# Network two with six steps of sevens: stores of outputs asked for a place later, gates ahead of low parts, casts for w_out's sums at other places

## The chip, the cores and the metric

The kernel runs on one core of one Trainium2 chip. The metric is device time in microseconds, from the first to the last instruction with what lies around them, as the median of several runs. A core has five engines with a queue each: TensorE (PE; its weight loads are shown as PEld), VectorE (DVE), ScalarE (ACT), GpSimd (POOL) and SyncE (SP, which here only issues DMAs). In the trace each engine's rows stand in the order in which the program gives them; engines wait for each other by semaphores.

## The reference

```python
def reference(**kwargs):
    ...
    x = attn_out            # X = fft(fft(x, axis=1), axis=2).real, x is 4 x 3072 x 256
    x = _moe_ref(x=x, **moe_kwargs)      # a gated network, width 1024
    x = x.reshape(B * S, x.shape[-1])
    return _moe2_ref(x=x, **moe2_kwargs)

def _moe2_ref(x, w_in, w_out):
    h = x @ w_in            # 12288 x 256 by 256 x 2048
    g = h - np.tanh(h)
    return (g @ w_out).astype(np.float32)   # 12288 x 2048 by 2048 x 256
```

The change touches the last of the three stages only, `_moe2_ref`, called network two here.

## The kernel before

The kernel runs in three stages: the transform, network one, network two. Every fp32 product is made of three fp32r matmuls (`mm3`, lines L395 to L397): high part by high, high by low, low by high. So each operand is split into a high part (a cast, `hi`, on ScalarE, L1081) and a low part (a subtraction, `lo`, on VectorE or GpSimd, L1083).

Network two works on 12 items `n` of 1024 tokens, and on each in 8 steps `q` of 256 hidden units. A step computes a 2x2 block of h by Strassen's scheme with seven products instead of eight: left operands `a11 a12 s1 s2 s3 a22 s4`, right operands in `TI`, all accumulating in four PSUM banks (two banks `x`, which alternate from step to step, one bank `z`, one bank `w`). The step then applies the gate h - tanh(h): `bend` is the tanh on ScalarE (L1072), and a subtraction on VectorE follows. Six of the eight steps, q = 0, 1, 3, 4, 6, 7, are "sevens": their product with w_out is made by seven products too (weights `W7`), which needs sums and differences of the gated blocks. The two others, q = 2 and 5, are plain (weights `WO`). In the last item q = 7 is plain too.

The order of all work is written out by hand in `step`. A step finishes its blocks 21 and 12 only while the next step runs; the leftovers are called by name through `late(...)`:

- `t21`, `g21`: tanh and gate of block 21, which lies in the old bank x. `c12`, `t12`, and `g12` or `G12`: the sum, tanh and gate of block 12, which lies in bank w.
- `l22`: the low part of block 22, read from bank z by VectorE. `f22`: a copy of the same block from bank z into SBUF by ScalarE (L1216).
- `s3`, `s1` (L1226): differences and sums with block 21 on VectorE; `s1` is added into the old bank x itself. `+s2`, `+s4` and `S4`: the other sums.
- `hs1`, `ls1` and so on, `ha12`, `LA12`: the high and low parts of those operands.

By what came before it a step has one of three forms. In form "b" both previous steps are sevens (q = 0, 1, 2, 5). In form "c" the previous step is plain (q = 3, 6). In form "e" the previous one is a seven and the one before it is plain (q = 4, 7). The steps q = 0 and 5 follow an "e"; q = 1 and 2 follow a "b". In the first item that `step` does, n = 1, q = 0 is a "c", q = 1 an "e" and q = 2 a "b". So there are 42 steps of form "b" in all: four in each of the items 2 to 11, two in item 1. Of these 20 follow a "b" and 22 an "e".

Early in each step the line `A.copy(Z, X)` (L1110) seeds bank z with the first product, and z must be free of the previous step's block 22 for it. In a "b" step the products `k1` (`apart`, tiles named `k`) are written into the previous step's bank x, which is free only once `s1`'s low part, `ls1`, has read it. Near the end of a step `V.tensor_add(Z, Wb, s3)` (L1180) makes block 22, and its tanh, gate and cast follow.

`fill()` stands four times in a step and runs what was put down for the next slot of a calendar: loads of `TI` for later steps (L1247, from `stream`), the left operands of the next item, the weights `W7` (`seven`: casts on ScalarE, L429, and six subtractions on GpSimd, L430 and L516 to L519). Item 1 begins at slot 32 of network two. Outputs are stored by `send` (L1034, a DMA of 256 KB on SP's queue), called by `part` and `whole_out`.

```python
        P(X, "s3")
        ...
        s3 = copied(X)
        ...
        P(Wb, "s1", True)
        ...
        V.tensor_add(Z, Wb, s3)
        t22 = bend(Z)
```

Of the kernel before, what the change touches and what calls it, by code (L numbers as in the profile page):

```python
# [406 lines left out]
class Kernel:  # L407
# [622 lines left out]
                self.V.tensor_add(self.acc[key], self.acc[key], K)  # L1030
        return add

    def send(self, n, t, h, a):
        self.nc.sync.dma_start(out=self.out[n, t, :, h], in_=a)  # L1034

    def part(self, n, t, h, eng=None):

# [19 lines left out]
    def step(self, n, q):  # L1057

        V, A, T, G = self.V, self.A, self.T, self.G
# [3 lines left out]
        seven = q in self.sevens(n)  # L1063
        one, two = (bool(p and p["seven"]) for p in (p1, p2))
        form = "b" if one and two else "c" if not one else "e"
        group = lambda p, o: [o, p] if p["q"] in (1, 4, 7) else [p]
        def P(ps, k, start=False):
            i = RIGHT[k]
            mm3(T, ps, [W[:, 0, i], W[:, 1, i]], [S[k][:, 0], S[k][:, 1]], start)
        def bend(src):  # L1070
            t = self.room(self.act, "c", "c", 4)
            A.activation(t, src, TANH)  # L1072
            return t
        def copied(src):
            t = self.room(self.act, "s", "s", 3)
            A.copy(t, src)  # L1076
            return t
        M, st = {}, {}
        def hi(k, src):
            M[k] = self.operand(k, *self.span(n, q, k))  # L1080
            A.copy(M[k][:, 0], src)  # L1081
        def lo(k, src, eng):
            eng.tensor_sub(M[k][:, 1], src, M[k][:, 0].bitcast(F32))  # L1083
        late = lambda *names: [p1["late"][k]() for k in names]
        new = lambda name: self.room(self.kp, "xt", name, 4)
        nop = lambda: None
        k1 = k2 = None
        if one and self.last(p1["n"], p1["q"]) == p1["q"]:
            g = group(p1, p2)
            k1, k2 = (lambda: self.apart(g, "a11")), (lambda: self.apart(g, "s1"))  # L1090
        if two and self.last(p2["n"], p2["q"]) == p2["q"]:
            g = group(p2, p3)
            k1, k2 = (lambda: self.apart(g, "s2")), (lambda: self.apart(g, "s3"))
        self.odd ^= 1
        X, Z = self.bank(f"x{self.odd}", "x"), self.bank("z", "z")
# [3 lines left out]
        elif form == "c":  # L1099
            self.whole(p1, "11", (0,))  # L1100
        P(X, "a11", True)
        if one:
            late("l22")
        late("t21")
        if form != "b":
            late("c12")
        if one:
            late("f22")
        late("g21")
        A.copy(Z, X)  # L1110
        if form == "b":
            self.direct(p2, "s4")
            if (n, q) == (1, 2):
                self.direct(p2, "a22")
            self.direct(p1, "a22")
            late("s3", "s1", "+s2", "hs3", "hs1", "c12", "t12")
        elif form == "c":
            self.whole(p1, "11", (1,))
            self.whole(p1, "22", (0,))
            late("t12", "h21", "g12")  # L1120
            if q == 3 and n > 1:
                self.part(n - 1, 1, 1)
            late("l21", "h12")
        else:
            self.whole(p2, "21")
            late("t12", "s3", "s1", "+s2", "hs1")
        P(Z, "a12")
        if form == "b":
            late("ls1", "ls3", "g12")
        elif form == "c":  # L1130
            late("l12")
        else:
            late("G12", "hs3", "ls3", "ls1", "ha12", "LA12")
        P(X, "s2")
        if form == "e":
            late("S4")
        t11 = bend(Z)
        s2 = copied(X)
        if form == "b":
            late("ha12", "la12", "+s4")  # L1140
        if q == 1 and n > 1:
            self.part(n - 1, 0, 0)
        if (n, q) == (1, 1):
            self.part(0, 1, 0)
            self.part(0, 1, 1, A.copy)
# [5 lines left out]
                self.direct(p1, "a22")  # L1151
            self.whole(p2, "12", (0,))
        add = k1() if k1 else nop
        if seven and form == "e":
            g = st["11"] = new("g11")
            V.tensor_sub(g, Z, t11)
            hi("a11", g)
            lo("a11", g, G)
        else:
            V.tensor_sub(Z, Z, t11)  # L1160
            hi("a11" if seven else "11", Z)
        add()
        P(X, "s3")
        if seven and form != "e":
            st["11"] = new("g11")
            A.copy(st["11"], Z)
        s3 = copied(X)
        if not (seven and form == "e"):
            lo("a11" if seven else "11", Z, V)
        if one:  # L1170
            late("hs2", "ls2")
        self.fill()
        Wb = self.bank("w", "w")
        P(Wb, "s1", True)
# [4 lines left out]
            self.whole(p2, "12", (1,))  # L1179
        V.tensor_add(Z, Wb, s3)  # L1180
        t22 = bend(Z)
        if one:
            late("hs4", "ls4")
        if q == 1 and n > 1:
            self.part(n - 1, 0, 1)
            self.whole_out(n - 1, 0, 1)
# [54 lines left out]
    def phase2(self):  # L1241
        A, V = self.A, self.V
        z0 = 16 * NP
        self.W7, self.C, self.acc, self.older, self.oldest = {}, {}, {}, None, None
        def stream(g):
            t = self.w1.tile([128, 2, 7, 128], F32R, tag="T", name="TI", bufs=4)
            self.nc.sync.dma_start(out=t.rearrange("p s k n -> p (s k n)").bitcast(F32), in_=self.ti[g % 8])  # L1247
            self.TI[g] = t
        for g in range(8, 8 * NP):
            self.at(z0 + 4 * (g - 1), lambda g=g: stream(g))  # L1250
        self.TI = dict(enumerate(self.TI))
        for j in range(3, 8):
            self.weights2(z0 + 4 * (j - 2), j, self.kp, "xt", 4)
        xt, ring = (self.kp, "xt", 4), (self.w1, "T", 4)
        t4 = (lambda: self.p2b, lambda: self.p2a)
        for i, (q, slot, src) in enumerate(((0, 24, xt), (1, 27, xt), (3, 30, xt), (4, 33, xt), (6, 36, (self.p2a, "wf", 1)), (7, 54, (self.p2a, "wf", 1)))):
            self.seven(z0 + slot, q, *((self.p2a, f"TI{i}", 1) if i < 4 else ring), *src, t4[i % 2])
        for n in range(NP):
            for q in range(8):
                if n == 0 and q == 1:  # L1260
                    self.xctx.close()
                    self.p2b = self.ctx.enter_context(self.tc.tile_pool(name="p2b", bufs=1, side="right", reuse_waits="tile"))
                    self.homes = [[self.p2a, "WO0", 1, 1.5], [self.p2a, "WO1", 1, 2.5], [self.p2a, "WO3", 1, 4.5], [self.w1, "WR", 1, 0.], [self.p2b, "M", 2, 1.], [self.p2b, "M", 2, 1.1],
                                  [self.wvp, "wv", 4, 5.6], [self.wvp, "wv", 4, 7.6], [self.wvp, "wv", 4, 9.8]] + [[self.act, "m", 4, t] for t in (8.3, 8.6, 9.3, 9.8)]
                if q == 1 and n + 1 < NP:
                    u = self.left2(n + 1)
                    names = "a11 a12 a22 +s1 +s3 +s2 +s4 s1 s3 s2 s4".split()
                    when = (7, 8, 11, 12, 12, 15, 16, 16, 19, 20, 22) if n == 0 else (12, 12, 13, 14, 14, 15, 24, 24, 25, 26, 27)
                    self.at(z0 + 32 * n + (8 if n else 5), u["load"])
                    for k, name in zip(when, names):  # L1270
                        self.at(z0 + 32 * n + k, u[name])
                if n:
                    self.step(n, q)
                else:
                    w2 = [[self.WO[q][:, s, 256 * c:256 * c + 256] for s in range(2)] for c in range(2)]
                    self.quad(2, n, q, 8, self.S2[n], self.TI.pop(q), w2, None)
                if (n, q) == (NP - 1, 3):
                    self.at(self.now + 1, *self.plain(7))
            if n == 0:
                self.pend["seven"] = False  # L1280
                self.C.update({(0, t, h): self.O[t][h] for t in range(2) for h in range(2)})
        p, w, n, G = self.pend, self.older, NP - 1, self.G
        late = lambda *names: [p["late"][k]() for k in names]
        a11, h, s2, t = (self.acc[n, k] for k in ("a11", "h", "s2", "t"))
        self.direct(w, "a12")
        K = self.bank(f"x{1 - self.odd}", "k")
        L = self.bank("z", "l")
        def extra(ps, k):
            a, m = self.product(w, k)
            mm3(self.T, ps, a, [m[:, 0], m[:, 1]])  # L1290
        extra(K, "s2")
        late("t21", "c12")
        V.tensor_add(s2, s2, K)
        V.tensor_add(t, t, K)
        late("t12", "g21")
        G.tensor_add(s2, s2, h)
        self.whole(p, "11")
        extra(L, "s3")
        late("h21", "g12", "l21", "h12", "l12")
        V.tensor_add(t, t, L)  # L1300
        self.whole(p, "22")
        G.tensor_add(h, h, t)
        self.direct(w, "s4")
        V.tensor_add(t, t, a11)
        self.whole(p, "21")
        for k, (i, a) in enumerate((((1, 0), t), ((1, 1), h), ((0, 0), a11), ((0, 1), s2))):
            if k == 2:
                self.whole(p, "12")
            V.tensor_add(a, a, self.C.pop((n, *i)))
            self.send(n, *i, a)  # L1310

    def plain(self, q):

# [115 lines left out]
```

## Time and profile before

| | before |
|---|---|
| median of 3 runs | 1671.08 us (1670.69 to 1671.22) |
| the profiled execution's own time | 1669.62 us |
| its span, first to last instruction | 1667.8 us |
| mean granted clock of TensorE | 0.998 |
| PE busy | 1616.8 us, 97% of the span |
| DVE, ACT, POOL busy | 82%, 77%, 67% |

The profiled execution is 1.46 us under the median of the runs, and 1.82 us of its time lie outside its span. Matmuls are pipelined, and a row's duration is longer than the distance to the next one; the busy share of PE therefore hides short waits. The count of matmuls in a stretch, or the distance from start to start, shows them. In the timeline views the columns are start, duration (both us), engine, line, operation, tiles written and read; in brackets the idle time of the engine before the row and what ended it.

### The profile page before, as it was taken

To read this page: it belongs to the slowest core of one execution; us is meant where nothing else is said; L and a number is where in the kernel's file an instruction comes from. 1 tells how busy PE (TensorE), PEld (TensorE's weight loads), DVE (VectorE), ACT (ScalarE), POOL (GpSimd) and SP (SyncE) were. 2 spreads that over 40 slices of the span, in tenths; PEclk is the share of its full clock that TensorE was granted. 3 is DMA by queue.
4 is the path that set the end of the run, shared out by engine and by line. 5 is a ranking of instruction groups with operands and counts; after the bars stand their busy time and mean duration, and the time that the engine had idled before them with its cause. 6 is when DMAs were issued, how large, how long until landed. Compare 5 with 4: busy or idle time off the path is not lost.

```text
span 1667.8 us, 22306 instructions
## 1 busy us (share of the span) xinstructions
PE 1616.8 (97%) x7283; PEld 1299.4 (78%) x7283; DVE 1360.9 (82%) x2115; ACT 1279.7 (77%) x2464; POOL 1111.4 (67%) x928
## 2 busy tenths in 40 slices
PE   8999999999999999999999999999999999999998
PEld 7978888888888887877777777777777777777776
DVE  7987888888898887777788878888788887888787
ACT  5887777777777777877878787878777878787875
POOL 1166667676666666767776767676767676767653
PEclk9999999999999999999999999999999999999999
DMA  9620111101111132444242424241414141414140
GB/s 334 170 58 26 46 45 64 34 30 57 52 58 64 45 108 90 176 137 144 79 149 77 151 75 153 73 155 69 159 67 161 67 161 67 162 66 161 67 164 26
DMA packets 59348, 168.74 MB, mean 101 GB/s; under 512 B 6864, under 2 KB 15824, under 8 KB 59232
## 3 DMA queue, kind: packets, MB, share of 16 engines
q1 hardware_dynamic: 57648, 162.87, 28.8%
q0 software_dynamic: 1440, 4.46, 1.6%
q8 instruction: 57, 0.93, 0.2%
q14 instruction: 59, 0.48, 0.1%
q10 hardware_dynamic: 144, 0.00, 0.0%
HBM read 128.43 MB, written 38.86 MB: 100 GB/s over the span
## 4 chain that ended last, share of the span: by engine, by line
PE 27%; DVE 16%; ACT 9%; DMA 2%; issue 1%; DVEq 0%; POOLq 0%; SPq 0%; ACTq 0%
ACT s L1081 4%; PE k L395 3%; PE k L397 3%; DVE a L1083 3%; PE k L396 3%; ACT a L1081 3%; DMA TI<-ti 2%; DVE g L1226 2%; PE x L395 2%; PE o L395 2%; PE o L397 2%; DVE x L1212 2%; PE o L396 2%; PE x L397 2%; PE x L396 2%; DVE z L1180 1%
## 5 line engine op out<-in xcount | busy, mean ns | idle before, releaser
L1083 POOL TENSOR_TENSOR s<-g,s 128x512 fp32r<-128x512 f32 x195 | 250.5, 1296 | 7.1 <-ACT s L1081 7.0
L1227 POOL TENSOR_TENSOR g<-g,g 128x512 f32<-128x512 f32 x107 | 138.7, 1296 | 113.4 <-DVE x L1226 67.6
L696 POOL TENSOR_TENSOR s<-xk,s 128x512 fp32r<-128x512 f32 x94 | 125.2, 1332 | 87.8 <-ACT s L694 82.7
L696 POOL TENSOR_TENSOR a<-xk,a 128x512 fp32r<-128x512 f32 x70 | 92.3, 1328 | 123.7 <-ACT a L694 123.6
L396 PE MATMUL o<-m,wv 128*128 128x512 f32 x384 | 149.7, 390 | 0.0
L397 PE MATMUL o<-m,wv 128*128 128x512 f32 x384 | 149.7, 390 | 0.0
L395 PE MATMUL o<-m,wv 128*128 128x512 f32 x384 | 149.6, 390 | 0.0
L1072 ACT ACTIVATE c<-z 128x512 f32<-128x512 f32 x176 | 105.5, 600 | 33.7 <-DVE z L1180 33.1
L1081 ACT CAST s<-g 128x512 fp32r<-128x512 f32 x195 | 120.9, 620 | 6.2 <-DVE g L1226 5.8
L1076 ACT COPY s<-x 128x512 f32<-128x512 f32 x176 | 104.2, 592 | 19.7 <-PE x L397 17.9
L1083 POOL TENSOR_TENSOR a<-g,a 128x512 fp32r<-128x512 f32 x64 | 82.8, 1294 | 39.9 <-ACT a L1081 39.8
L571 ACT ACTIVATE c<-z 128x512 f32<-128x512 f32 x112 | 67.2, 600 | 54.7 <-DVE z L660 54.5
L578 DVE TENSOR_TENSOR m<-z,m 128x512 fp32r<-128x512 f32 x112 | 76.8, 686 | 32.7 <-ACT m L576 32.7
L1192 DVE TENSOR_TENSOR z<-z,c 128x512 f32<-128x512 f32 x88 | 61.6, 700 | 46.3 <-ACT c L1072 44.6
L1083 DVE TENSOR_TENSOR a<-z,a 128x512 fp32r<-128x512 f32 x108 | 74.6, 691 | 24.3 <-ACT a L1081 14.7
L430 POOL TENSOR_TENSOR xr<-xt,xr 128x512 fp32r<-128x512 f32 x46 | 60.7, 1327 | 46.4 <-ACT xr L429 46.3
L395 PE MATMUL x<-s,TI 128*128 128x512 f32 x192 | 77.9, 406 | 13.6 <-ACT s L1076 13.3
L1180 DVE TENSOR_TENSOR z<-w,s 128x512 f32<-128x512 f32 x88 | 61.6, 700 | 35.6 <-ACT s L1076 26.3
L576 ACT CAST m<-z 128x512 fp32r<-128x512 f32 x112 | 65.8, 587 | 28.3 <-DVE z L664 23.5
L1081 ACT CAST a<-z 128x512 fp32r<-128x512 f32 x108 | 63.7, 590 | 29.9 <-DVE z L1192 23.2
L395 PE MATMUL x<-a,TI 128*128 128x512 f32 x192 | 76.9, 400 | 8.5 <-DMA TI<-ti 6.9
L396 PEld LDWEIGHTS o<-m,wv 128*128 128x128 f32 x384 | 72.1, 188 | 15.7 <-DVE m L578 0.5
(1019 smaller groups left out, 5815.0 us busy)
## 6 DMA issues: line engine op xcount, KB each, us to landing
TI<-ti SPq DMA_DIRECT2D x88, 896.0 KB, 5.5
spill<-r SPq DMA_DIRECT2D x48, 256.0 KB, 2.6
xk<-spill SPq DMA_DIRECT2D x48, 256.0 KB, 5.4
out<-o SPq DMA_DIRECT2D x44, 256.0 KB, 2.4
ti<-TI SPq DMA_DIRECT2D x8, 896.0 KB, 4.8
wf<-wf SPq DMA_DIRECT2D x17, 256.0 KB, 2.8
raw<-w_in SPq DMA_DIRECT2D x32, 128.0 KB, 2.2
cv<-w_out SPq DMA_DIRECT2D x16, 256.0 KB, 3.1
```

The lines of the kernel that those rows point to most:

```text
L395: T.matmul(ps, w[0], m[0], start=start, stop=False, skip_group_check=True)
L396: T.matmul(ps, w[0], m[1], start=False, stop=False, skip_group_check=True)
L397: T.matmul(ps, w[1], m[0], start=False, stop=stop, skip_group_check=True)
L571: A.activation(t, src, ACT.Tanh if ph == 2 else ACT.Relu)
L578: V.tensor_sub(M[blk][:, 1], g, M[blk][:, 0].bitcast(F32))
L696: eng.tensor_sub(S[name][:, 1], src(), S[name][:, 0].bitcast(F32))
L1072: A.activation(t, src, TANH)
L1076: A.copy(t, src)
L1081: A.copy(M[k][:, 0], src)
L1083: eng.tensor_sub(M[k][:, 1], src, M[k][:, 0].bitcast(F32))
L1180: V.tensor_add(Z, Wb, s3)
L1227: "+s2": lambda: G.tensor_sub(g("22"), g("22"), g("11")), "+s4": lambda: G.tensor_sub(g("12"), g("12"), g("22")),
```

## The change

The change does five things, all in network two.

1. `send` no longer issues its DMA at once; it puts it down for a later `fill()`, except for the last four outputs.
2. In form "b" the order `l22`, `t21`, `f22`, `g21` becomes `t21`, `g21`, `l22`, `f22`. So VectorE does block 21's gate ahead of block 22's low part.
3. In form "e" the high and low parts of `s1` are made after the gate and the casts of block 11, no longer at the head of the step; the cast `ha12` comes after the tanh of block 11; the gate of block 11 comes ahead of `LA12` and `S4`; and `hs4`, `ls4` change places with `hs2`, `ls2`.
4. The first part of an item's output, in q = 1, is added up after the sum of `k1` and no longer ahead of block 11's gate.
5. The six sets of `W7` are made at other slots: 23, 26, 29, 40, 45, 54 in place of 24, 27, 30, 33, 36, 54, and the fourth is loaded through another buffer.

```diff
-    def send(self, n, t, h, a):
-        self.nc.sync.dma_start(out=self.out[n, t, :, h], in_=a)
+    def send(self, n, t, h, a, now=False):
+        f = lambda: self.nc.sync.dma_start(out=self.out[n, t, :, h], in_=a)
+        f() if now else self.at(self.now + 1, f)
...
         P(X, "a11", True)
-        if one:
-            late("l22")
         late("t21")
-        if form != "b":
-            late("c12")
-        if one:
-            late("f22")
-        late("g21")
+        if form == "b":
+            late("g21", "l22", "f22")
+        elif form == "e":
+            late("l22", "c12", "f22", "g21")
+        else:
+            late("c12", "g21")
         A.copy(Z, X)
...
             self.whole(p2, "21")
-            late("t12", "s3", "s1", "+s2", "hs1")
+            late("t12", "s3", "s1", "+s2", "hs3", "ls3")
         P(Z, "a12")
...
-            late("G12", "hs3", "ls3", "ls1", "ha12", "LA12")
+            late("G12")
         P(X, "s2")
+        t11 = bend(Z)
+        side = seven and form == "e"
+        def gate():
+            if side:
+                st["11"] = new("g11")
+            V.tensor_sub(st["11"] if side else Z, Z, t11)
         if form == "e":
-            late("S4")
-        t11 = bend(Z)
-        s2 = copied(X)
+            late("ha12")
+            gate()
+            s2 = copied(X)
+            late("LA12", "S4")
+        else:
+            s2 = copied(X)
         if form == "b":
             late("ha12", "la12", "+s4")
-        if q == 1 and n > 1:
-            self.part(n - 1, 0, 0)
...
+        hi("a11" if seven else "11", st["11"] if side else Z)
+        if side:
+            lo("a11", st["11"], G)
+        if form == "e":
+            late("hs1", "ls1")
         add()
+        if q == 1 and n > 1:
+            self.part(n - 1, 0, 0)
         P(X, "s3")
...
-        if one:
+        if form == "b":
             late("hs2", "ls2")
+        elif form == "e":
+            late("hs4", "ls4")
...
-        if one:
+        if form == "b":
             late("hs4", "ls4")
+        elif form == "e":
+            late("hs2", "ls2")
...
-        for i, (q, slot, src) in enumerate(((0, 24, xt), (1, 27, xt), (3, 30, xt), (4, 33, xt), (6, 36, (self.p2a, "wf", 1)), (7, 54, (self.p2a, "wf", 1)))):
+        for i, (q, slot, src) in enumerate(((0, 23, xt), (1, 26, xt), (3, 29, xt), (4, 40, wf), (6, 45, wf), (7, 54, wf))):
```

How the built program's order changes is shown at three places. The first is VectorE in a "b" step that follows an "e", from block 22's sum (L1180 before, L1190 after) to the low part of `s1`. Tile a22 is the low part `l22`, the row that writes x from x and c is `g21`. Before, and then in the change:

```order
L1180 TENSOR_TENSOR z_12229<-w_12295,s_12290 128x512
L1192 TENSOR_TENSOR z_12229<-z_12229,c_12303 128x512
L1083 TENSOR_TENSOR a22_12309<-z_12229,a22_12309 128x512
L1212 TENSOR_TENSOR x_12228<-x_12228,c_12326 128x512
L1226 TENSOR_TENSOR g11_12282<-g11_12282,x_12228 128x512
L1226 TENSOR_TENSOR x_12228<-x_12228,g22_12328 128x512
L1209 TENSOR_TENSOR w_12295<-w_12295,s_12272 128x512
L1083 TENSOR_TENSOR s1_12343<-x_12228,s1_12343 128x512
```

```order
L1190 TENSOR_TENSOR z_12229<-w_12295,s_12290 128x512
L1204 TENSOR_TENSOR z_12229<-z_12229,c_12303 128x512
L1224 TENSOR_TENSOR x_12228<-x_12228,c_12325 128x512
L1084 TENSOR_TENSOR a22_12309<-z_12229,a22_12309 128x512
L1238 TENSOR_TENSOR g11_12266<-g11_12266,x_12228 128x512
L1238 TENSOR_TENSOR x_12228<-x_12228,g22_12329 128x512
L1221 TENSOR_TENSOR w_12295<-w_12295,s_12268 128x512
L1084 TENSOR_TENSOR s1_12343<-x_12228,s1_12343 128x512
```

The low part of block 22 now stands behind the gate of block 21; nothing else moved on VectorE here. ScalarE's order in a "b" step is the same in both programs: cast of a22, tanh `t21`, copy `f22`, the seed of z (L1110), casts of s3 and s1.

The second place is ScalarE in an "e" step, from the tanh `t12` (it reads w) to the tanh of block 22. Rows that write s from x are `copied(X)`, first after the product s2, then after the product s3. Before, and then in the change:

```order
L1072 ACTIVATE c_12247<-w_12193 128x512
L1081 CAST s1_12252<-x_12124 128x512
L1081 CAST s3_12258<-g11_12185 128x512
L1081 CAST a12_12262<-w_12193 128x512
L1072 ACTIVATE c_12270<-z_12229 128x512
L1076 COPY s_12272<-x_12228 128x512
L1081 CAST a11_12284<-g11_12282 128x512
L1076 COPY s_12290<-x_12228 128x512
L1081 CAST s2_12292<-g22_12237 128x512
L1072 ACTIVATE c_12303<-z_12229 128x512
```

```order
L1073 ACTIVATE c_12247<-w_12193 128x512
L1082 CAST s3_12252<-g11_12185 128x512
L1073 ACTIVATE c_12262<-z_12229 128x512
L1082 CAST a12_12264<-w_12193 128x512
L1077 COPY s_12268<-x_12228 128x512
L1082 CAST a11_12281<-g11_12266 128x512
L1082 CAST s1_12284<-x_12124 128x512
L1077 COPY s_12290<-x_12228 128x512
L1082 CAST s4_12292<-g12_12271 128x512
L1073 ACTIVATE c_12303<-z_12229 128x512
```

The cast of s1 moved from the head to behind the cast of a11, the tanh of block 11 moved ahead of the cast of a12, and s4 and s2 changed places.

The third place is SP's queue of DMA issues around q = 1 of an item; out is a store, TI a load of weights, xk a load of the next item. Before, and then in the change:

```order
L1247 DMA TI_12366<-ti 128x1792
L1034 DMA out<-o_12468 128x512
L1247 DMA TI_12471<-ti 128x1792
L1034 DMA out<-o_12511 128x512
L1034 DMA out<-o_12406 128x512
L1247 DMA TI_12578<-ti 128x1792
L916 DMA xk_12580<-spill 128x512
```

```order
L1259 DMA TI_12366<-ti 128x1792
L1259 DMA TI_12468<-ti 128x1792
L1034 DMA out<-o_12481 128x512
L1034 DMA out<-o_12510 128x512
L1259 DMA TI_12577<-ti 128x1792
L916 DMA xk_12579<-spill 128x512
L916 DMA xk_12581<-spill 128x512
L916 DMA xk_12583<-spill 128x512
L916 DMA xk_12585<-spill 128x512
L1034 DMA out<-o_12406 128x512
```

The first store of the item went behind the load of TI that it stood ahead of, and the third went behind the next load of TI and the four loads of xk.

## Rows read from the trace of the kernel before

**Rows 1.** Busy time in two stretches; counts in brackets, then clock, DMA share, GB/s.

```profile
300.00:400.00 100.00, 100.00 (x442) 82.32 (x441) 84.58 (x128) 74.74 (x139) 67.79 (x56) 1.00 0.16 51
...
1200.00:1300.00 100.00, 96.53 (x409) 74.85 (x408) 79.70 (x123) 79.62 (x148) 73.78 (x58) 1.00 0.33 111
```

**Rows 2.** Waits of TensorE over the whole run: total us, times, longest us.

```profile
PE x L395 <- ACT s L1076: 13.9, 24, 1.5
...
PE x L395 <- DMA TI<-ti: 6.9, 10, 2.1
```

**Rows 3.** Timeline of VectorE, an "e" step and three "b" steps, item around 1230 us.

```profile
1229.65 0.68 DVE L1222 TENSOR_TENSOR g<-w,g 128x512 f32<-128x512 f32 x1
...
1232.10 0.70 DVE L1180 TENSOR_TENSOR z<-w,s 128x512 f32<-128x512 f32 x1 [1.17 <-ACT s L1076]
...
1234.82 0.69 DVE L1083 TENSOR_TENSOR a<-z,a 128x512 fp32r<-128x512 f32 x1 [0.66 <-ACT a L1081]
1235.42 0.69 DVE L1212 TENSOR_TENSOR x<-x,c 128x512 f32<-128x512 f32 x1
...
1236.82 0.69 DVE L1226 TENSOR_TENSOR x<-x,g 128x512 f32<-128x512 f32 x1
...
1238.17 0.69 DVE L1083 TENSOR_TENSOR s<-x,s 128x512 fp32r<-128x512 f32 x1
...
1242.11 0.70 DVE L1180 TENSOR_TENSOR z<-w,s 128x512 f32<-128x512 f32 x1
...
1252.72 0.70 DVE L1180 TENSOR_TENSOR z<-w,s 128x512 f32<-128x512 f32 x1
```

**Rows 4.** Timeline of TensorE and its weight loads (PEld), the same stretch.

```profile
1229.09 0.39 PE L397 MATMUL o<-12_12149,WO 128*128 128x512 f32 x1
1230.04 0.50 PE L395 MATMUL x<-s,TI 128*128 128x512 f32 x1 [0.56 <-ACT s L1076]
...
1238.92 0.50 PE L395 MATMUL k<-a,W 128*128 128x512 f32 x1 [0.42 <-DVE s L1083]
...
1248.93 0.50 PE L395 MATMUL k<-s,W 128*128 128x512 f32 x1 [0.20 <-DVE s L1083]
...
1259.55 0.19 PEld L395 LDWEIGHTS k<-a,W 128*128 128x128 f32 x1 [0.40 <-DVE s L1083]
```

**Rows 5.** Timeline of ScalarE, the first of these "b" steps.

```profile
1234.68 0.61 ACT L1072 ACTIVATE c<-x 128x512 f32<-128x512 f32 x1
1235.60 0.59 ACT L1216 COPY g<-z 128x512 f32<-128x512 f32 x1 [0.31 <-DVE a L1083]
1236.22 0.57 ACT L1110 COPY z<-x 128x512 f32<-128x512 f32 x1
...
1237.55 0.59 ACT L1081 CAST s<-x 128x512 fp32r<-128x512 f32 x1
```

**Rows 6.** Line L1216, whole run: what ended ScalarE's idle time before it (us, times).

```profile
  DVE a L1083: 12.1, 42
```

**Rows 7.** Timeline of ScalarE, the "e" step ahead of them.

```profile
1227.42 0.59 ACT L1081 CAST s<-x 128x512 fp32r<-128x512 f32 x1 [0.84 <-DVE x L1226]
...
1229.38 0.60 ACT L1076 COPY s<-x 128x512 f32<-128x512 f32 x1
...
1231.49 0.58 ACT L1076 COPY s<-x 128x512 f32<-128x512 f32 x1
```

**Rows 8.** Timeline of SP, q = 1 of the same item.

```profile
1250.18 0.34 SPq L1034 DMA_DIRECT2D out<-o  x1
1250.61 0.38 SPq L1247 DMA_DIRECT2D TI<-ti  x1
```

**Rows 9.** Timelines of item 1, around its q = 1 and 2: VectorE, GpSimd, weight loads.

```profile
748.44 0.70 DVE L1180 TENSOR_TENSOR z<-w,s 128x512 f32<-128x512 f32 x1 [1.17 <-ACT s L1076]
...
753.17 1.31 POOL L430 TENSOR_TENSOR W<-t,W 128x512 fp32r<-128x512 f32 x1
...
756.91 0.19 PEld L395 LDWEIGHTS k<-a,W 128*128 128x128 f32 x1
```

More of the change, by code (lines that the diff above doesn't have):

```diff
@@ L1153, in step @@
         add = k1() if k1 else nop
[L1154 to L1161, printed above, removed]
+        if form != "e":
+            gate()
+        hi("a11" if seven else "11", st["11"] if side else Z)
[3 more added lines that the diff above has]
+            late("hs1", "ls1")
         add()
+        if q == 1 and n > 1:
+            self.part(n - 1, 0, 0)
         P(X, "s3")
-        if seven and form != "e":
+        if seven and not side:
             st["11"] = new("g11")
@@ L1167, in step @@
         s3 = copied(X)
-        if not (seven and form == "e"):
+        if not side:
             lo("a11" if seven else "11", Z, V)
-        if one:
+        if form == "b":
             late("hs2", "ls2")
+        elif form == "e":
+            late("hs4", "ls4")
         self.fill()
@@ L1253, in phase2 @@
             self.weights2(z0 + 4 * (j - 2), j, self.kp, "xt", 4)
-        xt, ring = (self.kp, "xt", 4), (self.w1, "T", 4)
+        xt, wf, ring = (self.kp, "xt", 4), (self.p2a, "wf", 1), (self.w1, "T", 4)
         t4 = (lambda: self.p2b, lambda: self.p2a)
-        for i, (q, slot, src) in enumerate(((0, 24, xt), (1, 27, xt), (3, 30, xt), (4, 33, xt), (6, 36, (self.p2a, "wf", 1)), (7, 54, (self.p2a, "wf", 1)))):
+        for i, (q, slot, src) in enumerate(((0, 23, xt), (1, 26, xt), (3, 29, xt), (4, 40, wf), (6, 45, wf), (7, 54, wf))):
             self.seven(z0 + slot, q, *((self.p2a, f"TI{i}", 1) if i < 4 else ring), *src, t4[i % 2])
@@ L1309, in phase2 @@
             V.tensor_add(a, a, self.C.pop((n, *i)))
-            self.send(n, *i, a)
+            self.send(n, *i, a, True)
     def plain(self, q):
```

## The prediction

> **What bounds the kernel now.** I read the stretches first. In network one TensorE starts 442 matmuls in 100 us, one each 0.226 us, and never waits; in network two it starts 409 in the same time [rows 1]. So in network two some 33 x 0.226 = 7.5 us of each 100 are lost, though TensorE looks 96.5% busy. Network two takes about 920 us, so about 65 us is all that a reordering can win, and any reordering can add to it.
>
> Then I looked for where the loss sits. The list of waits names two places: 24 waits of 0.58 us for a copy by ScalarE, in "e" steps, and 10 waits for a load of TI, in q = 2 [rows 2]. But a wait that is listed need not be the one that sets the pace, so I followed one item. Call T the start of block 22's sum (L1180) in a step, and K the first matmul into bank k in the next step if that is a "b". The three in a row are T = 1232.10, 1242.11, 1252.72 [rows 3] and K = 1238.92, 1248.93, 1259.55 [rows 4]. K - T is 6.82, 6.82 and 6.83 us, although TensorE lost time in quite different places between them. So K hangs on a chain of VectorE and ScalarE that starts at T, and each K row says what it waited for: VectorE's `ls1` [rows 4]. From K to the next T it is 3.19 and 3.79 us [rows 3, 4], TensorE's own work but for the output's part that VectorE does in q = 1. In a run of "b" steps the period is thus about 6.8 + 3.2 us, and the chain from T to K is the term to cost.
>
> The chain, in us after T = 1232.10: ScalarE's tanh `t21` runs from 2.58 to 3.19 [rows 5]. VectorE does `l22` from 2.72 to 3.41, `g21` from 3.32 to 4.01, `s1` from 4.72, `ls1` from 6.07 to 6.76 [rows 3], and K follows at 6.82. ScalarE's copy `f22` starts at 3.50, 0.09 after `l22` ended, the seed of z at 4.12, the cast of s1 at 5.45 to 6.04 [rows 5]; `ls1` waits for that cast by 0.03. `s1` needs `f22`, and `f22` waits for `l22`: 42 times, in every "b" step, ScalarE idles until just that row [rows 6].
>
> **Part 2, `g21` ahead of `l22` in "b" steps.** No work is added, but `l22` now queues behind an instruction that waits for `t21`. `g21` can start 0.03 after `t21` ends, at T + 3.22, only 0.10 earlier than before. VectorE's rows follow each other each 0.60 us (1234.82 to 1235.42 [rows 3]), so `l22` starts at 3.82 in place of 2.72 and ends at 4.51. Behind it wait `f22` (4.57), then the seed of z (0.62 later, 5.19), the casts of s3 and s1, `ls1` and K. In the trace the cast of s1 starts 1.33 after the seed of z [rows 5]; some 0.15 of that was a wait for s3 that would be gone, so it starts at 5.19 + 1.18 to 1.33 = 6.37 to 6.52 and ends 0.59 later; `ls1` takes 0.03 + 0.69, and K follows 0.06 after, at T + 7.7 to 7.9. So K - T grows by 0.87 to 1.06; I take 0.9, at the low end, since the wait for s3 should go. From K to the next T nothing changes, since all of that hangs on the same casts. TensorE will meet this as a wait for the seed of z, which is ready at 5.8, and a shorter one at K. For the 20 "b" steps that follow a "b" nothing comes back: 20 x 0.9 = **+18.0 us**.
>
> Here a page speaks against the change too. The Trainium skill, "PSUM — Partial Sum Buffer", section "PSUM bank collisions raise a hardware error", says that a read by ScalarE and a read by VectorE of one bank must not overlap, and that software has to order them by bank. The trace agrees: the copy starts 0.09 us after the low part ends, though neither writes the bank. By the page the +18.0 stands; were the two reads free to overlap, the first rival below would hold.
>
> **Part 3, the "e" steps.** Here ScalarE does the casts of s1, s3 and a12, the tanh and the copy of x in a row from 1227.42 to 1229.98 [rows 7]. TensorE could have gone on 0.23 after its row at 1229.09, at 1229.32, but starts at 1230.04 when the copy is done: 0.72 lost, and 0.11 more in the first matmul of the restart [rows 4]. With the cast of s1 (0.5 from row to row) gone from here, and the row of casts beginning earlier since s3 is made ahead of s1, the copy ends near 1229.3 and the wait closes. T moves by at least the 0.72. It moves by more if the copy that releases it moves by more [rows 3]: that copy ran from 1231.49 to 1232.07 [rows 7], though the product was out at about 1231.0 (1230.04, two more starts, one duration); so the most is 0.72 + 0.11 + 0.45 = 1.27. But ahead of it now stand two casts, a11 and s1, and `ls1` (0.69) is the last row on VectorE before T, behind `S4`, which stood at 1229.65 [rows 3]: with the product out at about 1230.2, copy and `ls1` end near 1231.1. I take T **1.0 earlier**, the middle. The "b" behind it gives back 0.9, so K there is only 0.1 earlier. There are 22 of these; for the 21 outside item 1's start: 21 x (-1.0 + 0.9) = **-2.1 us**. That `hs4`, `ls4` come first removes a wait of TensorE for `s4` in the same "b" step, but the time it frees is spent in the wait for the seed of z, so it counts nothing. In the very last step (an "e") the products `k1` need `ls1`, which now ends near 1231.2 on this item's clock, where TensorE wants it at 1229.32: +1.9, less the 0.72: **+1.2 us**.
>
> **Parts 1 and 4, stores and the output's part.** In q = 1 a store that waits for VectorE held SP until 1250.18, and the load of TI behind it went out at 1250.61 and came too late for q = 2 [rows 8]. That wait (ten of them, 6.9 us [rows 2]) will go. But in that step K comes 6.83 after T like in the others, so the wait lay inside the chain; removing it lengthens the wait at K and gains nothing: 0. The stores land late, but the buffers are written again some 10 us later, and the loads of xk that one store is moved behind are issued at once; 0. Moving the part behind `k1`'s sum leaves the same number of VectorE rows ahead of T: 0, at most 0.6 x 10 gained if VectorE had a gap there.
>
> **Part 5, and item 1.** In item 1 T was at 748.44 and the weights for k at 756.91, the matmul 0.23 later, 757.1, after a wait for TI of about 2 us [rows 2, 9]. With ScalarE free of two casts for W7 and the "e" order above, T is near 747.5; the load is no longer late; K is at 747.5 + 7.7 = 755.2: **-1.9 us**. W7's work on GpSimd (a row is 1.31 [rows 9], a set has six, some 4 us) moves for two sets from the first two steps of item 1 to its steps 2 and 3, where GpSimd also makes the next item's operands. What is queued behind are the sums `+s2` that `S4` waits for. Between 0 and 3 us; I take **+1.0**, nearer to 0 since it is one step of one item.
>
> **Sum.** 18.0 - 2.1 + 1.2 - 1.9 + 1.0 = +16.2 us. The profiled execution took 1669.62, so 1685.8; the median of the runs is 1.46 above it, at 1671.08, so the time forecast is **1687 us**, slower by 1.0%. With the bounds: 0.87 to 1.06 in 41 steps gives -1.2 to +6.6 us, T of the "e" at 0.72 to 1.27 gives +5.9 to -5.7, the part -6, GpSimd -1 to +2. Not all at one end: 1679 to 1694.
>
> **The rivals.**
> *Faster: the chain from T to K hardly grows.* Were `f22` not held by `l22`, VectorE's six rows from `g21` at 3.22 would put `ls1` at 6.22 and K at 6.95, 0.13 later than now. Then the 1.0 of the "e" steps stays: 20 x 0.13 - 21 x 0.87 + 1.2 - 2.7 + 1.0 = -16.2, **1655 us**. It decides at a growth of about 0.5 per "b" step (41 x 0.5 = 21 x 1.0). For it speak the listed waits, which are just what the change aims at; against it all 42 rows in which ScalarE waits for `l22` [rows 6]. 0.12.
> *No change.* The growth is near 0.5, since part of `l22`'s delay is hidden, by an earlier s3 or by T coming yet earlier: **1671 us**, 0.07.
> *Slower, but less.* T in "e" steps comes 1.27 earlier and the part in q = 1 frees VectorE's gap: 16.2 - 5.7 - 5 = +5.5, **1677 us**, 0.13.
> *Slower still.* GpSimd falls behind in item 1 and the "e" steps give only 0.72: 16.2 + 5.9 + 2 = +24, **1695 us**, 0.05.
> The forecast itself, 1679 to 1694: 0.63.
>
> **How the numbers follow.** The range leaves out the faster rival and half of the unchanged one below, and most of the last one above: 1673 to 1694. A difference of 0.2% (3.3 us) is about what a measurement of this kernel can tell from none. Faster 0.12; same 0.07; slower 0.13 + 0.05 + 0.63 = 0.81.
>
> **What would show it.** In the profile after: K - T near 7.7 in every "b" step; `f22` right behind `l22`, and `l22` behind `g21`; TensorE's waits for the seed of z (L1110) up from almost nothing to 30 us or more, those for the copy (L1076) down from 13.9 to under 3, those for TI down to 1 or none; matmuls in a stretch of 100 us down to about 402. The prediction is wrong if K - T stays under 7.3, or if T in the "e" steps comes earlier by much more than 1.0.

## The result, and the profile after

| | before | after |
|---|---|---|
| median, 4 runs each | 1670.88 us (1670.1 to 1671.22) | 1680.57 us (1679.99 to 1681.21) |
| the profiled execution | 1669.62 us, span 1667.8 | 1681.21 us, span 1679.4 |

The ratio is 1.0059 (95% interval 1.0041 to 1.0076): the change makes the kernel slower by about 9.7 us by the medians, 11.6 by the two profiled executions. The forecast was 1687 us, range 1673 to 1694.

Busy time in the stretch of network two shows it first; it had 409 matmuls [rows 1]:

```profile
1200.00:1300.00 100.00, 95.87 (x401) 73.47 (x401) 78.74 (x124) 77.99 (x146) 73.05 (x58) 1.00 0.34 115
```

TensorE's waits over the whole run (total us, times, longest us):

```profile
PE z L395 <- ACT z L1110: 23.3, 43, 1.0
PE o L396 <- DVE a L1084: 7.3, 21, 0.5
...
PE w L395 <- DVE g L1234: 2.5, 1, 2.5
PE k L395 <- DVE s L1084: 1.4, 1, 1.4
PE x L395 <- ACT s L1077: 1.0, 2, 0.7
```

The two waits that stood there before [rows 2] are gone, 13.9 us to 1.0 and 6.9 to none. In their place stand a wait for the seed of bank z, 43 times (once before, 1.1 us), and one for the low part of block 22, 21 times. The wait at K is down to one place; the same list of before had there

```profile
PE k L395 <- DVE s L1083: 10.7, 31, 0.4
```

so TensorE waits for the same chain now, but at an earlier place in it.

The chain from T to K in one "b" step behind an "e", VectorE first (it answers to rows 3; the last two rows are the next two T):

```profile
1236.66 0.70 DVE L1190 TENSOR_TENSOR z<-w,s 128x512 f32<-128x512 f32 x1 [0.28 <-PE w L397]
...
1239.88 0.70 DVE L1224 TENSOR_TENSOR x<-x,c 128x512 f32<-128x512 f32 x1 [1.15 <-ACT c L1073]
1240.49 0.68 DVE L1084 TENSOR_TENSOR a<-z,a 128x512 fp32r<-128x512 f32 x1
...
1241.88 0.70 DVE L1238 TENSOR_TENSOR x<-x,g 128x512 f32<-128x512 f32 x1
...
1243.51 0.69 DVE L1084 TENSOR_TENSOR s<-x,s 128x512 fp32r<-128x512 f32 x1 [0.33 <-ACT s L1082]
...
1247.37 0.70 DVE L1190 TENSOR_TENSOR z<-w,s 128x512 f32<-128x512 f32 x1
...
1258.66 0.70 DVE L1190 TENSOR_TENSOR z<-w,s 128x512 f32<-128x512 f32 x1
```

ScalarE in the same step (rows 5 before):

```profile
1239.25 0.60 ACT L1073 ACTIVATE c<-x 128x512 f32<-128x512 f32 x1
1241.26 0.59 ACT L1228 COPY g<-z 128x512 f32<-128x512 f32 x1 [1.41 <-DVE a L1084]
1241.88 0.57 ACT L1110 COPY z<-x 128x512 f32<-128x512 f32 x1
1242.36 0.62 ACT L1082 CAST s<-g 128x512 fp32r<-128x512 f32 x1
1242.88 0.59 ACT L1082 CAST s<-x 128x512 fp32r<-128x512 f32 x1
```

TensorE and its weight loads: the seed's wait in this step, and K in this "b" and the two behind it (rows 4 before):

```profile
1242.50 0.50 PE L395 MATMUL z<-a,TI 128*128 128x512 f32 x1 [0.54 <-ACT z L1110]
...
1244.25 0.19 PEld L395 LDWEIGHTS k<-a,W 128*128 128x128 f32 x1 [0.53 <-DVE s L1084]
...
1254.96 0.19 PEld L395 LDWEIGHTS k<-s,W 128*128 128x128 f32 x1 [0.52 <-DVE s L1084]
...
1266.25 0.19 PEld L395 LDWEIGHTS k<-a,W 128*128 128x128 f32 x1 [0.52 <-DVE s L1084]
```

Here the first matmul of k starts with its weight load, so K - T is 7.59, 7.59 and 7.59; it was 6.82. The reader is to see three things. The low part (1240.49) stands behind the gate (1239.88), and the gate gained nothing: it starts 3.22 after T in place of 3.32. ScalarE, free at 1239.85, idles 1.41 for that low part and copies only then. And the last three rows of ScalarE follow each other 0.48 and 0.52 apart, closer than before. The line of that copy shows the wait 43 times, in all 42 "b" steps (1.41 each) and once in item 1's "e" step:

```profile
  DVE a L1084: 59.5, 43
```

It was 12.1 us in 42 times [rows 6].

### The profile page after: what moved, and what is told of

Read it like the earlier page. It is cut to its first block, busy times and chain, and to the rows that moved or that the text cites. A ratio compares the mean times of both kernels' runs of the same rounds, so it can differ in the third digit from the quotient of the medians.

```text
span 1679.4 us, 22346 instructions
## 1 busy us (share of the span) xinstructions
PE 1625.0 (97%) x7283; PEld 1298.8 (77%) x7283; DVE 1355.0 (81%) x2115; ACT 1276.3 (76%) x2464; POOL 1112.9 (66%) x928
## 4 chain that ended last, share of the span: by engine, by line
PE 33%; ACT 10%; DVE 9%; issue 1%; POOL 1%; DVEq 0%; POOLq 0%; ACTq 0%
PE k L395 4%; PE k L397 3%; PE k L396 3%; ACT c L1073 3%; PE o L395 3%; PE o L397 3%; PE o L396 3%; PE x L395 3%; PE x L397 3%; PE x L396 3%; ACT s L1082 3%; PE w L395 2%; DVE x L1224 2%; DVE s L1084 2%; DVE z L1190 2%; DVE z L1204 2%
## 5 line engine op out<-in xcount | busy, mean ns | idle before, releaser
L1084 POOL TENSOR_TENSOR a<-g,a 128x512 fp32r<-128x512 f32 x64 | 83.0, 1298 | 13.9 <-ACT a L1082 13.7
L1224 DVE TENSOR_TENSOR x<-x,c 128x512 f32<-128x512 f32 x88 | 61.2, 695 | 36.3 <-ACT c L1073 36.3
L396 PEld LDWEIGHTS o<-m,wv 128*128 128x128 f32 x384 | 72.1, 188 | 15.7 <-DVE m L578 0.5
L395 PEld LDWEIGHTS o<-m,wv 128*128 128x128 f32 x384 | 72.1, 188 | 15.2
L397 PEld LDWEIGHTS o<-m,wv 128*128 128x128 f32 x384 | 72.1, 188 | 15.1
L1228 ACT COPY g<-z 128x512 f32<-128x512 f32 x65 | 38.0, 585 | 59.5 <-DVE a L1084 59.5
```

Source lines behind the costliest of these rows:

```text
L395: T.matmul(ps, w[0], m[0], start=start, stop=False, skip_group_check=True)
L396: T.matmul(ps, w[0], m[1], start=False, stop=False, skip_group_check=True)
L397: T.matmul(ps, w[1], m[0], start=False, stop=stop, skip_group_check=True)
L1224: do = dict(t21=t21, c12=c12, t12=t12, g21=lambda: V.tensor_sub(X, X, st["t21"]))
```

## The experiments

Times are medians; a ratio is against the kernel before, run beside it, with its 95% interval. Theory A is the prediction's: the late low part holds the copy, the seed and all up to K, and the earlier T of the "e" steps pays only part of it back.

**1 and 2: part 2 undone alone, and done alone.**

```diff
-        late("t21")
-        if form == "b":
-            late("g21", "l22", "f22")
+        if form == "b":
+            late("l22")
+        late("t21")
+        if form == "b":
+            late("f22", "g21")
```

> The changed kernel, with part 2 alone undone: in form b the low part of block 22 stands ahead of the tanh and the gate of block 21 again. Theory A (the late low part holds the copy f22, the seed of z and all up to K): K - T falls from 7.59 to 6.8 in every b step and the time by 42 x 0.77 = 32 us, to about 1648. Theory B (the growth comes from the stores, the e steps or GpSimd, and the b order only shows where the wait is listed): K - T stays near 7.5 and the time between 1675 and 1681. Theory C (TensorE's own work or the load of TI takes over as soon as the chain is shorter): K - T near 6.8, but from K to the next T it grows, and the time is 1655 to 1668.

Measured: 1649.44 us, ratio 0.9878 (0.9864 to 0.9891). T on VectorE, and the next K on TensorE:

```profile
1219.51 0.70 DVE L1192 TENSOR_TENSOR z<-w,s 128x512 f32<-128x512 f32 x1 [0.29 <-PE w L397]
```

```profile
1226.32 0.50 PE L395 MATMUL k<-a,W 128*128 128x512 f32 x1 [0.42 <-DVE s L1084]
```

K - T is 6.81, as before the change. So without part 2 the change would have made the kernel faster by 1.2%.

> The kernel before, with part 2 alone done: in form b the order t21, g21, l22, f22. Theory A: K - T 7.59 in every b step, 42 x 0.77 = 32 us more, about 1703; the waits for TI in q = 2 disappear into the longer chain. Theory B (part 2 alone does little): 1671 to 1676. Theory C (the waits that TensorE has anyway in the e steps and for TI swallow part of it): 1685 to 1697.

Measured: 1701.16 us, ratio 1.0187 (1.0173 to 1.02); K - T is 7.59 and 30.9 us are lost, 0.74 for each of 42 steps. In time and K - T both results are those of theory A; the "e" steps and the stores have no share in the growth. One thing that theory A said in 2 did not happen: the waits for TI stay, 7.1 us in 11 places. In those steps too, but for item 1's, K - T is 7.59, so they lie inside the longer chain, as they lay inside the shorter one.

**3: part 3 alone.** The "e" branches of the diff, in the kernel before.

> The kernel before, with part 3 alone done: the e steps' order, all else as before. Theory A (block 22's sum comes about 0.95 earlier in each e step, and the b step behind it passes this on): 22 x 0.95 = 21 us less, about 1650. Theory B (the gain is only lent, and the b step behind waits for something that did not move): 1666 to 1671. The prediction's own sum would give 22 x 1.0 less 1.2 for the last step: 1650 too.

Measured: 1651.24 us, ratio 0.9898 (0.9883 to 0.9914), 19 us less: theory A. It is not the full 21: item 1's "e" step gives nothing, since TensorE waits 3.3 us for TI behind it in place of 2.1, and the very last step is 1.0 longer. Parts 2 and 3 nearly add: 1670.3 + 30.9 - 19.0 = 1682, and the whole change takes 1680.6. That leaves about -1.6 us for parts 1, 4 and 5 together; 4 and 5 were not run alone.

**4: part 1 alone.**

```diff
-    def send(self, n, t, h, a):
-        self.nc.sync.dma_start(out=self.out[n, t, :, h], in_=a)
+    def send(self, n, t, h, a, now=False):
+        f = lambda: self.nc.sync.dma_start(out=self.out[n, t, :, h], in_=a)
+        f() if now else self.at(self.now + 1, f)
```

> The kernel before, with part 1 alone done: stores asked for a place later. Theory A (the wait for TI in q = 2 lies inside the chain from T to K): TensorE's waits for TI go from 10 to 0 or 1, the wait for ls1 at K in q = 2 grows by as much, and the time stays within 2 us of 1671. Theory B (the wait for TI counts): 10 x 0.69 = 6.9 us less, about 1664. Theory C (a store that lands late holds a tile back): over 1673.

Measured: 1668.77 us, ratio 0.9991 (0.9982 to 0.9999). TensorE's waits for TI are gone from the list, and the wait at K rose from 10.7 us in 31 places to

```profile
PE k L395 <- DVE s L1084: 14.6, 41, 0.4
```

So of the 6.9 us of waiting 3.9 moved to K, in ten more places: theory A. Another 2.1 are item 1's. There K had stood 8.69 after T, beyond the chain, so its wait of 2.1 for TI did count; but when it goes, another stands in its place, and K is still 8.17 after T:

```profile
753.29 0.50 PE L396 MATMUL o<-s,W 128*128 128x512 f32 x1 [1.51 <-POOL s L1084]
```

The profiled executions differ by 0.6 us, the medians by 1.5, a small gain that theory A did not hold.

**5 and 6: who holds whom at bank z.** In the changed kernel the copy goes ahead of the low part; in the second case both stand ahead of `t21` too.

```diff
-            late("g21", "l22", "f22")
+            late("g21", "f22", "l22")
```

> The changed kernel with one exchange in form b: the copy f22 ahead of the low part l22 (t21, g21, f22, l22). Theory A (the cost of part 2 is that ScalarE's copy and the seed stand in a row behind the late low part; two engines read bank z one after the other, in the order of the program): f22 starts right behind t21, at T + 3.2, the low part behind the copy at T + 3.9, the seed at T + 4.65 in place of 5.22; then s1, its cast and its low part bring K to T + 7.2, so 42 x 0.39 = 16 us less than the changed kernel, about 1664. Theory B (what costs is the low part's place behind the gate on VectorE, whatever ScalarE does): K - T stays 7.59 and the time 1680. Theory C (the two reads of bank z may overlap): the low part starts before the copy ends, at T + 3.8.

Measured: 1662.45 us, ratio 0.995 (0.9937 to 0.9962), K - T 7.11. That is near theory A, and not B. Two rows of ScalarE, the copy right behind the tanh and the seed behind the low part:

```profile
1239.35 0.59 ACT L1228 COPY g<-z 128x512 f32<-128x512 f32 x1
1240.88 0.57 ACT L1110 COPY z<-x 128x512 f32<-128x512 f32 x1 [0.94 <-DVE a L1084]
```

The low part stays behind the gate here, and yet 18 us of the loss are gone against the changed kernel. So the place on VectorE is not the whole cost: 0.48 of the growth of 0.77 came with the copy's turn behind the low part. The other 0.29 are left, since the seed, which writes bank z, still waits 0.94 for that low part. Theory C can't be judged here: VectorE comes to the low part at 1240.10, when the copy has ended (1239.94).

```diff
-        late("t21")
         if form == "b":
-            late("g21", "l22", "f22")
+            late("f22", "l22")
+        late("t21")
+        if form == "b":
+            late("g21")
```

> The changed kernel with the order f22, l22, t21, g21 in form b, so that nothing but bank z can hold the low part: f22 should start behind the cast of a22, near T + 2.6. Theory A (two engines' reads of one bank follow each other): the low part, which starts at T + 2.72 in the kernel before, starts only when the copy ends, near T + 3.25; the gate g21 comes at T + 3.85, half a microsecond later than in the kernel before, since t21 stands behind f22, and K - T is 7.2 to 7.4: 1664 to 1672. Theory C (the reads may overlap): the low part starts at T + 2.72, the gate at T + 3.75, K - T 7.1 to 7.2: 1660 to 1664.

Measured: 1669.95 us, ratio 0.9995 (0.9986 to 1.0004), K - T 7.31: theory A. ScalarE's copy and then VectorE's low part of the same block:

```profile
1233.21 0.59 ACT L1230 COPY g<-z 128x512 f32<-128x512 f32 x1
```

```profile
1233.84 0.69 DVE L1084 TENSOR_TENSOR a<-z,a 128x512 fp32r<-128x512 f32 x1 [1.14 <-ACT g L1230]
```

Neither reads what the other writes, and VectorE had been idle for 1.14 us; still the low part starts 0.04 after the copy ends (1233.80). The two reads of bank z follow each other in the program's order, whichever is first. The Trainium skill, "PSUM — Partial Sum Buffer", section "PSUM bank collisions raise a hardware error", asks the program to keep two engines' accesses to one bank apart by semaphores, reads too. The traces agree with that in both orders; what the chip does with overlapping reads was not tried here.

**7 and 9: part 3 in two pieces.** In 7 only `hs1`, `ls1` move behind the cast of block 11. In 9 only the tanh and gate of block 11 move ahead.

```diff
-            late("t12", "s3", "s1", "+s2", "hs1")
+            late("t12", "s3", "s1", "+s2")
...
-            late("G12", "hs3", "ls3", "ls1", "ha12", "LA12")
+            late("G12", "hs3", "ls3", "ha12", "LA12")
...
             hi("a11" if seven else "11", Z)
+        if form == "e":
+            late("hs1", "ls1")
         add()
```

> The kernel before with a piece of part 3 alone: in e steps the high and low part of s1 are made behind the cast of block 11; the tanh of block 11 still stands behind the cast of a12, and hs4 and hs2 in the old order. Theory A (the wait of 0.58 for the copy of x is made by the row of ScalarE's casts, and the cast of s1 is one of them): the copy comes 0.5 earlier, block 22's sum too, 22 x 0.5 = 11 us less, about 1660. Theory B (the whole gain of the e steps hangs on the cast of s1): 1651. Theory C (the tanh's and the gate's places make the gain): 1670.

Measured: 1676.62 us, ratio 1.0036 (1.0022 to 1.005). No theory held: slower, by 6 us. ScalarE's row in an "e" step, from the cast of a12 to the second copy of x; then TensorE's restart, and VectorE's last rows up to T:

```profile
1229.70 0.59 ACT L1081 CAST a<-w 128x512 fp32r<-128x512 f32 x1 [0.59 <-DVE w L1230]
...
1230.67 0.59 ACT L1076 COPY s<-x 128x512 f32<-128x512 f32 x1
1232.24 0.62 ACT L1081 CAST a<-g 128x512 fp32r<-128x512 f32 x1 [0.97 <-DVE g L1156]
1232.77 0.58 ACT L1081 CAST s<-x 128x512 fp32r<-128x512 f32 x1
1233.24 0.59 ACT L1076 COPY s<-x 128x512 f32<-128x512 f32 x1
```

```profile
1231.32 0.50 PE L395 MATMUL x<-s,TI 128*128 128x512 f32 x1 [0.16 <-ACT s L1076]
```

```profile
1233.38 0.69 DVE L1083 TENSOR_TENSOR s<-x,s 128x512 fp32r<-128x512 f32 x1 [1.17 <-ACT s L1081]
1233.99 0.69 DVE L1182 TENSOR_TENSOR z<-w,s 128x512 f32<-128x512 f32 x1
```

Part of the room that the cast of s1 leaves at the head becomes a wait of 0.59 for the gate of block 12, since the cast of a12 is next. Still TensorE restarts 0.55 behind its row before (1230.77), not 0.95 [rows 4], so 0.40 are won there. They are lost behind it: between the copies the cast now stands in the way, so that they are 2.57 apart, not 2.11 [rows 7], and the low part of s1 comes last before T. From the restart to T it is 2.67, not 2.06 [rows 3, 4]. So the distance to T from the T ahead of it is 0.21 longer (11.57 for 11.36; in q = 4 it is 0.14 longer), some 3.5 us in all. As much again comes from the very last step, which is 3.8 us longer: K waits 3.0 for the late low part there, where the longest such wait was 0.4.

```profile
PE k L395 <- DVE s L1083: 13.7, 32, 3.0
```

> The kernel before with the other piece of part 3 alone: in e steps the tanh and the gate of block 11 come first, ahead of the cast of a12, its low part and S4, while the high and low part of s1 stay at the head of the step. Theory A (two waits have to go: the copy after the product s2 is held by the row of casts, that after s3 by the late gate and cast of block 11): the first copy stays where it was, since as many casts stand ahead of it, the second comes 0.45 earlier, and 22 x 0.45 = 10 us go, about 1660; only both pieces together give the 0.95 per step. Theory B (part 3's gain hangs on the tanh and gate alone): about 1651. Theory C (without the cast of s1 gone nothing is won): 1668 to 1672.

Measured: 1672.41 us, ratio 1.0013 (1.0004 to 1.0022): theory C. The first copy stayed, the second came 1.68 after it in place of 2.11 [rows 7], as theory A said, and yet T did not move: TensorE's restart to T is 2.09, as 2.06 before [rows 3, 4]. TensorE, then VectorE:

```profile
1232.39 0.50 PE L395 MATMUL x<-s,TI 128*128 128x512 f32 x1 [0.56 <-ACT s L1077]
...
1233.42 0.51 PE L395 MATMUL w<-s,TI 128*128 128x512 f32 x1
...
1233.99 0.40 PE L397 MATMUL w<-s,TI 128*128 128x512 f32 x1
```

```profile
1232.68 0.68 DVE L1234 TENSOR_TENSOR g<-w,g 128x512 f32<-128x512 f32 x1
1234.48 0.70 DVE L1190 TENSOR_TENSOR z<-w,s 128x512 f32<-128x512 f32 x1 [1.12 <-ACT s L1077]
```

The list names the copy, which had ended at 1233.98. What came last is the product in bank w, whose last row starts at 1233.99 and takes 0.40; and that product had started 0.06 after S4, which reads bank w and now stands behind the gate, was done (1233.36). The line of S4 says who waited for it over the whole run, in all 23 "e" steps:

```profile
  PEld w L395: 11.4, 23
```

T follows the end of that row by 0.09, as in the changed kernel, where the list does name TensorE. So a copy that comes earlier than T's other input wins nothing, and only both pieces together do. The 2 us that the run is slower by lie in item 1, where TensorE waits 3.7 us for TI in place of 2.1 and the T of q = 2 comes 2.5 later (762.63 for 760.12).

**8: the faster version.** The changed kernel without part 2, with sets five and six of `W7` later and the very last step as before.

```diff
-            late("t12", "s3", "s1", "+s2", "hs3", "ls3")
+            late("t12", "s3", "s1", "+s2", *(("hs1", "ls1") if end else ()), "hs3", "ls3")
...
-        if form == "e":
+        if form == "e" and not end:
             late("hs1", "ls1")
...
-(6, 45, wf), (7, 54, wf)
+(6, 50, wf), (7, 55, wf)
```

> The changed kernel with part 2 undone and two small repairs: the fifth and sixth set of W7 at slots 50 and 55 in place of 45 and 54, and s1's cast and low part at the head of the step again in the very last step alone. Theory A (in item 1 the sum S4 waits 2.5 us behind W7's subtractions on GpSimd; in the last step TensorE waits 1.4 us for the late ls1): against the changed kernel without part 2 (1649.4 us) 2.5 and 1.4 us less, about 1645.5, and both waits gone from the list. Theory B (other work of GpSimd, the next item's left operands, holds that sum): the wait of 2.5 us stays, 1648.

Measured: 1645.82 us, ratio 0.985 (0.9837 to 0.9864), faster than both kernels. Both waits are off the list: theory A. In the stretch of 100 us it starts 423 matmuls:

```profile
1200.00:1300.00 100.00, 98.47 (x423) 78.07 (x422) 81.94 (x127) 81.93 (x151) 72.23 (x58) 1.00 0.34 114
```

## Why the prediction was right, step by step

**Part 2, right in its mechanism, too large in its size.** The copy was forecast at T + 4.57 and starts at 4.60; the seed at 5.19, it is 5.22. The cast of s1 was put 1.18 to 1.33 behind the seed, and comes 1.00 behind it (1241.88 to 1242.88). The prediction read this distance off the kernel before as ScalarE's own, but for a wait of 0.15; there the cast of s1 had been VectorE's to set, since the sum s1 ended at 1237.51 and the cast started at 1237.55 [rows 3, 5]. With both inputs ready, as now, the casts follow each 0.48 and 0.52. So K - T is 7.59, not 7.7, a growth of 0.77 and not 0.9. (By the forecast's own rows K would come at 7.74 to 7.89, which is 0.92 to 1.07 more than 6.82; its 0.87 to 1.06 is a slip of the sum.) The Trainium skill, "ScalarE: Activation LUTs", section "What ACT_TABLE_LOAD costs", says that ACTIVATEs back to back overlap by about 93 ns. A copy and a cast here, 0.57 and 0.62 long, agree, with 0.09 and 0.10 of overlap.

"From K to the next T nothing changes" was not quite so: in q = 0 a further 0.07 went (1244.25 to 1247.37 is 3.12, it was 3.19 [rows 3, 4]). Here too bank z decides. The last row of VectorE before T, block 11's low part, starts 0.04 after ScalarE's copy of that block has ended, at 1246.55 behind a copy from 1245.92 (before: 1241.29 behind 1240.66), and with ScalarE's rows closer together this copy starts 1.67 after K in place of 1.74. Per "b" step 0.74 remain, by experiments 1 and 2 (31.1 and 30.9 us in 42 steps), and 41 x (0.9 - 0.74) = 6.6 us is the error of this term. TensorE's wait for the seed was put at 30 us or more; it is 23.3, and 7.3 stand at the low part, which the prediction did not name.

**Part 3, right in its size, by a mended reason.** The gap from the T ahead of it to the "e" step's own T was 11.36, up to 1232.10 [rows 3], and is 10.44, up to 1236.66. The earlier T of before, and of after:

```profile
1220.74 0.70 DVE L1180 TENSOR_TENSOR z<-w,s 128x512 f32<-128x512 f32 x1
```

```profile
1226.22 0.70 DVE L1190 TENSOR_TENSOR z<-w,s 128x512 f32<-128x512 f32 x1
```

That is 0.92 for the forecast 1.0; in q = 4 it is 0.99 (11.40 to 10.41). TensorE's restart, and its product in bank w behind it:

```profile
1234.80 0.40 PE L395 MATMUL x<-s,TI 128*128 128x512 f32 x1
```

```profile
1235.61 0.19 PEld L395 LDWEIGHTS w<-s,TI 128*128 128x128 f32 x1 [0.38 <-DVE g L1234]
```

The first source is all there: from the T ahead of it the restart comes 0.72 earlier (8.58 for 9.30), as forecast. But it needs the tanh moved ahead as well as the cast of s1 out of the row (experiment 7). The second source, an earlier second copy, gives 0.20, from the restart to T 1.86 for 2.06; and what comes last is neither the copy nor the low part of s1, which the prediction named, but the product in bank w, which starts 0.06 after S4 (1235.55) and which the line of T names 21 times:

```profile
  PE w L397: 6.5, 21
```

The same product is why the second source was not to be had alone (experiment 9).

**Parts 1 and 4.** Nothing was forecast; part 1 alone gives 1.5 us by the medians, 0.6 by the profiles. Part 4 was not run alone.

**Item 1 and the end.** T in item 1 comes 1.17 earlier, at 747.27 for 748.44 [rows 9], near the forecast 747.5, and K at 754.85, forecast at 755.2. GpSimd cost more than the +1.0 taken: in item 1's q = 4 the sum S4 waits for `+s2`, which stands behind a set of `W7` and the next item's operands. VectorE, and GpSimd:

```profile
779.35 0.69 DVE L1234 TENSOR_TENSOR g<-w,g 128x512 f32<-128x512 f32 x1 [2.46 <-POOL g L1239]
781.16 0.70 DVE L1190 TENSOR_TENSOR z<-w,s 128x512 f32<-128x512 f32 x1 [0.52 <-ACT s L1082]
```

```profile
769.92 1.01 POOL L430 TENSOR_TENSOR W<-wf,W 128x384 fp32r<-128x384 f32 x1
...
776.81 1.28 POOL L706 TENSOR_TENSOR xk<-xk 128x512 f32<-128x512 f32 x1
778.05 1.26 POOL L1239 TENSOR_TENSOR g<-g,g 128x512 f32<-128x512 f32 x1
```

So 2.5 us, within the 0 to 3 that were named. Experiment 8 moved the set away and the wait went. In the very last step `ls1` holds K, as forecast, for 1.4 us and not 1.9; the step grew by 0.9, not 1.2.

**The sum.** In the profiles: 16.2 forecast, less 6.6 for the "b" steps, plus 0.9 for the "e" steps (their mean is 0.955, so 21 x 0.045), plus 1.5 for GpSimd, less 0.3 for K in item 1 and 0.3 at the end, is 11.4; measured 11.6. The time forecast, 1687, is 6.7 us too long, and only 4.6 of them are terms of the sum. The other 2.1 are the step from profile to median: the profiled execution was taken to lie 1.46 below the median, and of the changed kernel it lies 0.64 above. (The 65 us named as all that a reordering can win are 69 by their own numbers, 7.5 in each 100 of 920; nothing hangs on it.) The faster rival fell with its condition (the copy is held by the low part in all 42 "b" steps). Experiment 1 gives the time with no growth at all, 1649 us; the rival's 1655 has 0.13 of growth in 41 steps, some 5 us.

## What to carry to other kernels

When a waiting instruction is moved ahead of one that could run, ask who is held by the second: here a gate that gained 0.1 us pushed a low part back by 1.1, and a copy and a seed of another engine with it, because they use the same bank in turn. Cost the whole chain to the next step's wait; count back-to-back rows from start to start, not by their durations, and read that distance where no row of them waits for an input. And try a bundle of moves in pieces: one of five cost 31 us and hid a gain of 20 in the others, while the two halves of the best piece were each worth nothing or less.

## What the runs showed that was not expected

Moving one cast out of a full row of ScalarE (experiment 7) made the kernel slower by 6 us: the next instruction in the queue was not ready, so the row gave back 0.40 and not 0.72, and at its new place the cast and its low part cost 0.61, and 3.8 us in the last step. A wait put down to the copy (experiment 9, 1.12 us) had in truth ended with TensorE, 0.5 us after that copy was done. And two stores that stand on SP for 5.54 us cost nothing: the load of TI behind them went out at 1263.60, and TensorE's list has no wait for TI. SP's rows:

```profile
1257.95 5.54 SPq L1034 DMA_DIRECT2D out<-o  x2
1263.60 0.37 SPq L1259 DMA_DIRECT2D TI<-ti  x1
```
